# The u half of x times w_in as seven block products, with x kept whole in float32

## The chip, the cores and the metric

The kernel runs on one core of a Trainium2 chip. The metric is the device time of one execution in microseconds (us). The kernel before takes 490.66 us, the median of three runs from 490.58 to 491.45. The profile is one more execution, which took 491.71 us, of which the traced span is 489.9 us.

## The reference

An attention without a softmax over the products gives x, and a gated feed-forward block with a spatial gate takes x on. There are 8 batches (b), 576 positions, 8 heads of 64 channels (512 in all), and a hidden width of 1024, which splits into a u half and a v half of 512.

```
q = softmax(q, channels);  k = softmax(k, positions)
x[b] = q (k^T v)                         # [576, 512], heads side by side
h = gelu_tanh(x @ w_in)                  # w_in [512, 1024]
u, v = h[:, :512], h[:, 512:]
v_n = (v - mean(v)) / sqrt(var(v) + 1e-6) * g_ln
v_s = w_sg @ v_n + b_sg                  # over positions, w_sg [576, 576]
out = x + (u * v_s) @ w_out              # w_out [512, 512]
```

## The kernel before, in words

Every large product runs in TensorE's fp32r type and keeps float32's precision by splitting each operand into a high part (rounded to fp32r) and a low part (the rest): high x high, low x high and high x low are summed in PSUM. A product thus costs three passes.

All of x, u and the output lie transposed, channels on partitions, positions along the free axis. Per batch, the steps are:

- `x_kv b` (L685): x of batch b from its q and k^T v, into three PSUM tiles, and then k^T v of batch b+1 (`kv_all`). ACT's `x_high` casts x from PSUM to its high part, DVE's `x_low` subtracts that from PSUM and leaves the low part. `x_h` and `x_l` have two buffers each, so that two batches may be in flight.
- `hv_mm b i` (L747): one 128-row tile of the v half, 12 matmuls of 512 columns. There are nine of these for each pair of batches: the last 64 rows of two batches share the fifth tile of the even one. Then `hv_gelu`, `hv_sq`, `hv_stat`, `hv_pow`, `hv_norm` and the split `hv_high`, `hv_low`.
- `hu_mm b f` (L813), four of them: a 128-row tile of the u half, 4 blocks of 128 input channels x 3 passes x 2 halves of 288 positions = 24 matmuls of 128x288. `hu_gelu` follows on ACT.
- `sg_mm b d` (L821), four of them, 28 matmuls of 128x288; `gate` (DVE) multiplies with u, `gate_high` (ACT) and `gate_low` (DVE or POOL) split the result.
- `out_mm b e` (L850), four of them, 24 matmuls of 128x288. `out_add` (DVE, L856) adds the high part of x from the PSUM result into a tile `o`, `out_rest` (DVE or POOL, L862) adds the low part, `out_store` sends it off.

Beside this run the softmaxes of q and k of later batches (`q_max` to `q_turn`, `k_sub`, `k_exp`, `kt_max`) on DVE, ACT and POOL, and, in batch 0 and 1 only, a finer start-up form of the same steps and the splitting of the weights (`wi_*`, `ws_*`, `wo_*`).

What sets the order is a text, `PLAN` (L34 to L131): steps are issued one by one in its order, and each engine keeps the order in which it was given its instructions. An engine that waits for one instruction therefore holds back all that is behind it. Two-bank PSUM tiles (`ps2`, three of them) go round among x, u, sg and out results, one-bank tiles (`ps1`, two) among v tiles and k^T v. All matmuls are issued by one helper (L238), all other instructions by another (L151), so rows are told apart by tile names.

Of the kernel before, what the change touches and what calls it, by code (L numbers as in the profile page):

```python
# [957 lines left out]
```

## Time and profile before

| what | value |
|---|---|
| median of 3 runs | 490.66 us (490.58 to 491.45) |
| the profiled execution | 491.71 us, traced span 489.9 us |
| PE busy | 483.5 us, 99% of the span |
| DVE, ACT, POOL busy | 334.8 us (68%), 240.3 us (49%), 162.2 us (33%) |
| granted TensorE clock | 0.999 of full speed, mean |

The page names the busy time of each engine, then the span in 40 slices, the chain that ended last and the costliest groups. PE is busy in all but the first and the last slice. What an instruction of a group takes is its mean; its record can overlap with that of the instruction behind it, so the spacing of starts is less than the mean.

### The profile page before, as it was taken

How to read it: one execution, taken by the hardware profiler on the slowest of the kernel's cores; microseconds unless marked ns; L12 is line 12 of the kernel's file. 1: busy time of each engine (PE TensorE's matmuls, PEld its weight loads, DVE VectorE, ACT ScalarE, POOL GpSimd, SP SyncE). 2: the span in 40 equal slices, each digit the busy share in tenths (PEclk: the TensorE clock that was granted, in tenths of full speed). 3: DMA queues.
4: the chain of work that ended last, by engine and by line, in shares of the span. 5: the costliest groups of instructions: out<-in, count | busy, mean ns of one | idle time of the engine just before them, and what ended most of it. 6: DMA issues, size and time to landing. Idle time of an engine off the chain costs nothing.

```text
span 489.9 us, 9391 instructions
## 1 busy us (share of the span) xinstructions
PE 483.5 (99%) x3885; PEld 446.9 (91%) x3885; DVE 334.8 (68%) x530; ACT 240.3 (49%) x398; POOL 162.2 (33%) x173
## 2 busy tenths in 40 slices
PE   8999999999999999999999999999999999999997
PEld 6698789999899889998899989999899979999997
DVE  8999898788578875896666687586156663426162
ACT  4899777732645657354625583356415154221220
POOL 4214423662425242751442701333023320114030
PEclk9999999999999999999999999999999999999999
DMA  8995741454147231544802243114000010000102
GB/s 301 359 403 217 277 118 65 143 199 105 63 141 286 80 131 47 160 136 161 251 27 98 98 135 118 30 74 128 0 27 0 25 74 0 1 2 24 50 25 97
DMA packets 20637, 57.28 MB, mean 117 GB/s; under 512 B 3057, under 2 KB 3569, under 8 KB 20594
## 3 DMA queue, kind: packets, MB, share of 16 engines
q1 hardware_dynamic: 20594, 56.68, 33.9%
q8 instruction: 30, 0.49, 0.4%
q14 instruction: 13, 0.11, 0.1%
HBM read 47.22 MB, written 9.45 MB: 116 GB/s over the span
## 4 chain that ended last, share of the span: by engine, by line
PE 92%; DVE 4%; ACT 2%; issue 1%; DMA 1%; POOL 0%; ACTq 0%
PE ps L238 92%; DVE o L151 1%; DVE vnl L151 1%; DMA qq<-q 1%; ACT qq L151 1%; DVE wi_l L151 0%; ACT qs L151 0%; DVE qm L151 0%; ACT x_l L151 0%; DVE qq L151 0%; POOL qq L151 0%; ACT o L151 0%; DVE wi_h L151 0%; DVE qd L151 0%; DVE qt L151 0%
## 5 line engine op out<-in xcount | busy, mean ns | idle before, releaser
L151 DVE TENSOR_TENSOR u<-ps,u 128x576 f32<-128x576 f32 x32 | 24.1, 754 | 57.3 <-PE ps L238 48.6
L151 ACT CAST gh<-u 128x576 fp32r<-128x576 f32 x32 | 21.1, 675 | 78.1 <-DVE u L151 78.0
L238 PE MATMUL ps<-ulow,wo_h 128*128 128x288 f32 (+1 forms) x260 | 56.5, 295 | 0.0
L238 PE MATMUL ps<-gh,wo_l 128*128 128x288 f32 (+1 forms) x260 | 56.4, 294 | 0.0
L238 PE MATMUL ps<-gh,wo_h 128*128 128x288 f32 (+1 forms) x260 | 56.3, 294 | 0.0
L238 PE MATMUL ps<-ws_h,vnl 128*128 128x288 f32 x256 | 54.9, 296 | 0.7 <-DVE vnl L151 0.7
L238 PE MATMUL ps<-ws_h,vnh 128*128 128x288 f32 x256 | 55.0, 296 | 0.0
L238 PE MATMUL ps<-ws_l,vnh 128*128 128x288 f32 x256 | 54.9, 296 | 0.0
L151 ACT ACTIVATE u<-ps 128x576 f32<-128x576 f32 (+2 forms) x36 | 21.0, 599 | 63.9 <-PE ps L238 59.7
L151 POOL TENSOR_TENSOR ulow<-u,gh 128x576 fp32r<-128x576 f32 x16 | 24.2, 1516 | 72.6 <-DVE ulow L151 43.7
L151 POOL TENSOR_TENSOR rs<-ve,half 128x1 f32<-128x1 f32 x36 | 27.9, 780 | 50.6 <-DVE ve L151 50.2
L238 PEld LDWEIGHTS ps<-gh,wo_h 128*128 128x128 f32 x260 | 42.4, 188 | 0.7
L238 PE MATMUL ps<-x_h,wi_h 128*128 128x288 f32 (+2 forms) x256 | 41.9, 299 | 0.3 <-ACT x_l L151 0.3
L238 PEld LDWEIGHTS ps<-ws_h,vnl 128*128 128x128 f32 x256 | 41.3, 188 | 0.9 <-DVE vnl L151 0.9
L238 PEld LDWEIGHTS ps<-gh,wo_l 128*128 128x128 f32 x260 | 42.1, 188 | 0.0
L238 PEld LDWEIGHTS ps<-ws_h,vnh 128*128 128x128 f32 x256 | 41.6, 188 | 0.5
L238 PEld LDWEIGHTS ps<-ulow,wo_h 128*128 128x128 f32 x260 | 42.0, 189 | 0.0
L238 PEld LDWEIGHTS ps<-ws_l,vnh 128*128 128x128 f32 x256 | 41.3, 188 | 0.0
L238 PE MATMUL ps<-x_h,wi_l 128*128 128x288 f32 (+2 forms) x256 | 41.3, 296 | 0.0
L238 PE MATMUL ps<-x_l,wi_h 128*128 128x288 f32 (+2 forms) x256 | 41.2, 296 | 0.0
L151 ACT ACT_TABLE_LOAD x30 | 38.5, 1283 | 5.4 <-DMA qq<-q 3.9
L151 DVE SCALAR_TENSOR_TENSOR vnl<-v,rs,vnh 128x512 fp32r<-128x512 f32 x32 | 30.9, 972 | 14.9 <-ACT vnh L151 14.7
(119 smaller groups left out, 1038.0 us busy)
## 6 DMA issues: line engine op xcount, KB each, us to landing
vv<-v SPq DMA_DIRECT2D x16, 650.0 KB, 5.2
out<-o SPq DMA_DIRECT2D x31, 288.0 KB, 3.1
qq<-q SPq DMA_DIRECT2D x14, 576.0 KB, 4.2
kk<-k SPq DMA_DIRECT2D x12, 640.0 KB, 5.7
kmt<-kt SPq DMA_DIRECT2D x24, 288.0 KB, 3.9
ghws<-w_sg SPq DMA_DIRECT2D x5, 320.0 KB, 8.4
kmt<-scr SPq DMA_DIRECT2D x6, 256.0 KB, 4.2
ukt<-kt SPq DMA_DIRECT2D x4, 288.0 KB, 6.5
```

The lines of the kernel that those rows point to most:

```text
L151: ins = op(*args, **kw)
L238: tc.keep_in_program_order(nc.tensor.matmul(*args, **kw))
```

## The change

It has four parts.

First, from batch 2 on the u half is no longer four `hu_mm` but seven block products in Winograd's form of Strassen's method. x (512 channels x 576 positions) and the u half of w_in (512 x 512) are cut in 2 x 2 blocks. Four sums of weight blocks are formed once, while batch 1 runs (`sw_get`, `sw_add`, `sw_high`, `sw_low`), and four sums of x blocks for each batch (`d_add` on DVE, `d_high` on ACT, `d_low` on DVE). `us_mm b n` (n = 1 to 7) is one product of 2 x 2 x 3 = 12 matmuls of 128x288, each with its own stationary operand. Products 1 and 2 add up in PSUM tile `ua`, 5 and 3 in `uc`, and 6, 7 and 4 in `ub`. DVE's `us_add` reads `ub` after product 6, after 7 and after 4, and `uc` after 5 and after 3, each time before the next product is added on top. `us_one` (ACT) copies product 1 before product 2 goes on top. Four `us_gelu` follow instead of four `hu_gelu`.

Second, x is copied from PSUM to a float32 tile `xf` (`x_get`, `x_tail`, ACT; two buffers, by the parity of the batch), and `x_high` and `x_low` work from that tile. `out_add` adds the output into `xf` in place, `out_rest` and `both` are gone, and the store reads `xf`. The high and low parts of x have one buffer each. For batch 0, `x_sum` forms `xf` from the two parts.

Third, the memory for this comes from other tiles: the x sums live in `u` (whole), in `gh`, `qq` and a new tile `sd` (parts); `sd` also holds the weight sums and half of what `gate_low` writes. Odd batches no longer have their last 64 positions in front.

Fourth, `PLAN` is new from its row 14 on.

```diff
-hv_pow 3 0, q_top 5 0, out_store 1 2, out_mm 2 2, load_kt 6 1, out_add 2 2, out_rest 2 2 V, load_kt 6 2, kt_max 6 1, load_kt 6 3, hu_mm 3 1
...
+d_low 3 1, x_get 4 1, us_mm 3 1, q_turn 5 0, us_mm 3 6, hv_stat 3 2 A, d_high 3 3, d_low 3 3, us_one 3, d_low 3 4, hv_pow 3 2, hv_high 3 2, us_mm 3 5
...
-    x_h, x_l = (slots(n, 2, [P, NP, S + TL], F32R) for n in ("x_h", "x_l"))
-    u_s = slots("u", 5, [P, S])
+    xx_h, xx_l = (sb(n, [P, NP, S + TL], F32R) for n in ("x_h", "x_l"))
+    xf_s = [sb(f"xf{i}", [P, NP, S]) for i in range(2)]
+    uu_s = slots("u", 2, [P, 2, S])
...
-    sq = sb("sq", [P, DV])
...
-    o_all = sb("o", [P, ST, S])
...
+    def xf(b):
+        return xf_s[b % 2]
+    def u_s(b, f, at=None):
+        return uu_s(b, f // 2, at=f // 2)[:, f % 2]
+    def sd_all():
+        return late("sd", [P, 12 * DH + 4 * HS])
...
+    def x_get(b, h, E=A):
+        copy(E, xf(b)[:, 2 * h:2 * h + 2, 0:ST * P], st[f"x{h}", b])
+    def x_tail(b, E=A):
         ps = st["xt", b][:, :, 0:2 * TL].rearrange("p z (h n) -> p z h n", h=2)
-        yield ps, x_tile(x, b)[:, :, where(b)[1]].rearrange("p (h z) n -> p z h n", z=2)
-        if b % 2:
-            yield ps, x(b - 1)[:, :, S:S + TL].rearrange("p (h z) n -> p z h n", z=2)
+        copy(E, xf(b)[:, :, ST * P:S].rearrange("p (h z) n -> p z h n", z=2), ps)
...
+    def x_sum(h, E=V):
+        hs = slice(2 * h, 2 * h + 2)
+        E.tensor_tensor(out=xf(0)[:, hs], in0=f32(xx_h[:, hs, 0:S]), in1=f32(xx_l[:, hs, 0:S]), op=ALU.add)
     def x_high(b, h):
-        ps, to = x_main(x_h, b, h)
-        A.copy(out=to, in_=ps)
-    def x_low(b, h):
-        (ps, to), (_, hi) = x_main(x_l, b, h), x_main(x_h, b, h)
-        V.tensor_tensor(out=to, in0=ps, in1=f32(hi), op=ALU.subtract)
+        hs, n = slice(2 * h, 2 * h + 2), S if b > 1 else ST * P
+        A.copy(out=xx_h[:, hs, 0:n], in_=xf(b)[:, hs, 0:n])
+    def x_low(b, h, E=V):
+        hs, n = slice(2 * h, 2 * h + 2), S if b > 1 else ST * P
+        E.tensor_tensor(out=xx_l[:, hs, 0:n], in0=xf(b)[:, hs, 0:n], in1=f32(xx_h[:, hs, 0:n]), op=ALU.subtract)
...
     def x_endh(b):
-        for ps, to in x_ends(x_h, b):
-            A.copy(out=to, in_=ps)
-    def x_endl(b):
-        for (ps, to), (_, hi) in zip(x_ends(x_l, b), x_ends(x_h, b)):
-            V.tensor_tensor(out=to, in0=ps, in1=f32(hi), op=ALU.subtract)
...
+    def w_parts(n):
+        if n == 3:
+            return w_block(1, 0)
+        z = sd_all()[:, 0:12 * DH].rearrange("p (k t c n) -> p k t c n", k=3, t=2, c=2)
+        return [z[:, {1: 0, 2: 1, 4: 2}[n], t] for t in range(2)]
...
+    def sw_add(n, E=V):
+        a, b, op = {
+            1: (w_whole(1, 0), w_whole(1, 1), ALU.add),
+            2: (w_sum(1), w_whole(0, 0), ALU.subtract),
+            3: (w_whole(0, 0), w_whole(1, 0), ALU.subtract),
+            4: (w_whole(0, 1), w_sum(2), ALU.subtract),
+        }[n]
+        E.tensor_tensor(out=w_sum(n), in0=a, in1=b, op=op)
...
+    def d_parts(b, n):
+        if n == 1:
+            z = sd_all()[:, 12 * DH:].rearrange("p (t c n) -> p t c n", t=2, c=2)
+        elif n == 3:
+            z = qq_s("d", b, n, at=1, shape=[P, 2, 2, HS], dt=F32R)
+        else:
+            z = gh_s("d", b, n, at=n // 2 - 1, shape=[P, 2, 2, HS])
+        return [z[:, t] for t in range(2)]
...
+    def d_sum(b, n):
+        return uu_s("d", b, n % 2, at=n % 2, shape=[P, 2, 2, HS])[:, (n - 1) // 2]
+    def d_add(b, n, E=V):
+        x, y = {
+            1: lambda: (x_block(b, 0, 1), x_block(b, 0, 0)),
+            2: lambda: (x_block(b, 1, 1), d_sum(b, 1)),
+            3: lambda: (x_block(b, 1, 1), x_block(b, 0, 1)),
+            4: lambda: (x_block(b, 1, 0), d_sum(b, 2)),
+        }[n]()
+        E.tensor_tensor(out=d_sum(b, n), in0=x, in1=y, op=ALU.subtract)
+    def d_high(b, n):
+        A.copy(out=d_parts(b, n)[0], in_=d_sum(b, n))
+    def d_low(b, n, E=V):
+        hi, lo = d_parts(b, n)
+        E.tensor_tensor(out=lo, in0=d_sum(b, n), in1=f32(hi), op=ALU.subtract)
...
+    def us_mm(b, n):
+        def xs(i, j):
+            return [block(z, j, i, HS) for z in (xx_h, xx_l)]
+        l, r, name, first = {
+            1: (w_block(0, 0), xs(0, 0), "ua", True),
+            2: (w_block(0, 1), xs(1, 0), "ua", False),
+            3: (w_parts(4), xs(1, 1), "uc", False),
+            4: (w_block(1, 1), d_parts(b, 4) if n == 4 else None, "ub", False),
+            5: (w_parts(1), d_parts(b, 1) if n == 5 else None, "uc", True),
+            6: (w_parts(2), d_parts(b, 2) if n == 6 else None, "ub", True),
+            7: (w_parts(3), d_parts(b, 3) if n == 7 else None, "ub", False),
+        }[n]
+        if first:
+            bank(ps2, name, b)
+        for s in range(2):
+            fs, m = slice(s * P, s * P + P), 0
+            for p, q in ((0, 0), (1, 0), (0, 1)):
+                for c in range(2):
+                    mm(st[name, b][:, s, 0:HS], l[p][:, c, fs], r[q][:, c], start=first and m == 0, stop=m == 5, skip_group_check=not first)
+                    m += 1
+    def u_block(b, i, j):
+        return uu_s(b, i, at=i)[:, :, j * HS:j * HS + HS]
...
+    def us_add(b, n, E=V):
+        of, one, to = {
+            6: ("ub", (1, 0), (0, 1)), 5: ("uc", (1, 0), (1, 1)), 7: ("ub", (1, 1), (1, 1)),
+            3: ("uc", (0, 1), (0, 1)), 4: ("ub", (1, 0), (1, 0)),
+        }[n]
+        E.tensor_tensor(out=u_block(b, *to), in0=us_sum(b, of), in1=u_block(b, *one), op=ALU.add)
+    def us_gelu(b, i, j):
+        z = u_block(b, i, j)
+        A.activation(z, z if i or j else us_sum(b, "ua"), AF.Gelu_apprx_tanh)
...
+    def gate_rest(b, d):
+        if d < 2:
+            return sd_all()[:, 12 * DH + d * S:12 * DH + d * S + S]
+        return uu_s("low", b, at=0, dt=F32R)[:, d - 2]
...
+        E.tensor_tensor(out=gate_rest(b, d), in0=u_s(b, d), in1=f32(gated(b, d)), op=ALU.subtract)
...
     def out_add(b, e):
-        if b == B - 1:
-            V.tensor_tensor(out=split(o_s(b, e)), in0=st["o", b, e][:, :, 0:HS], in1=split(o_s(b, e)), op=ALU.add)
-            return
-        V.tensor_tensor(out=split(o_s(b, e, at=4 * b + e)), in0=st["o", b, e][:, :, 0:HS], in1=f32(split(x_h(b)[:, e, 0:S])), op=ALU.add)
-    def out_rest(b, e, E=G):
-        o = o_s(b, e)
-        E.tensor_tensor(out=o, in0=o, in1=f32(x_l(b)[:, e, 0:S]), op=ALU.add)
+        o = split(xf(b)[:, e])
```

Three places in the order of the instructions. On PE, batch 3, where the u half is computed (`x_h`, `x_l` are the parts of x, `wi_h`, `wi_l` those of w_in, `ghd_3_2` and `qqd_3_3` the x sums 2 and 3, `sd` the weight sums and x sum 1); before:

```order
L238 MATMUL ps2_0_78<-ulow_2_3_2369,wo_h_853 128x288 x2
L238 MATMUL ps2_0_78<-gh2_1_2363,wo_l_854 128x288 x2
L238 MATMUL ps2_1_79<-x_h3_2010,wi_h_61 128x288 x8
L238 MATMUL ps2_1_79<-x_h3_2010,wi_l_62 128x288 x8
L238 MATMUL ps2_1_79<-x_l3_2027,wi_h_61 128x288 x8
L238 MATMUL ps2_2_80<-x_h3_2010,wi_h_61 128x288 x8
L238 MATMUL ps2_2_80<-x_h3_2010,wi_l_62 128x288 x8
L238 MATMUL ps2_2_80<-x_l3_2027,wi_h_61 128x288 x8
```

and now, products 1, 6, 5 and the start of 7:

```order
L246 MATMUL ps2_0_80<-x_h_74,wi_h_61 128x288 x2
L246 MATMUL ps2_0_80<-x_h_74,wi_l_62 128x288 x2
L246 MATMUL ps2_0_80<-x_l_75,wi_h_61 128x288 x2
L246 MATMUL ps2_0_80<-x_h_74,wi_h_61 128x288 x2
L246 MATMUL ps2_0_80<-x_h_74,wi_l_62 128x288 x2
L246 MATMUL ps2_0_80<-x_l_75,wi_h_61 128x288 x2
L246 MATMUL ps2_1_81<-ghd_3_2_2541,sd_1062 128x288 x12
L246 MATMUL ps2_2_82<-sd_1062 128x288 x12
L246 MATMUL ps2_1_81<-qqd_3_3_2660,wi_h_61 128x288 x2
L246 MATMUL ps2_1_81<-qqd_3_3_2660,wi_l_62 128x288 x2
L246 MATMUL ps2_1_81<-qqd_3_3_2660,wi_h_61 128x288 x4
L246 MATMUL ps2_1_81<-qqd_3_3_2660,wi_l_62 128x288 x2
```

The two groups of 24 matmuls that stood in two PSUM tiles became groups of 12, with a second product going on top of the first in `ps2_1_81`.

On DVE at the same place (`kmt` is the k of batch 6, `vnl` and `v3` belong to the v half, `o` is the output tile); before:

```order
L151 TENSOR_TENSOR o_77<-ps2_0_78,x_h2_1625 128x576
L151 TENSOR_TENSOR o_77<-o_77,x_l2_1630 128x576
L151 TENSOR_REDUCE ktall_6_2501<-kmt_6_1_2536 128x1
L151 BN_STATS s63_1_2662<-v3_1_2387 128x6
L151 BN_AGGR mv3_1_2663<-s63_1_2662 128x2
L151 TENSOR_SCALAR ve3_1_2666<-mv3_1_2663 128x1
L151 SCALAR_TENSOR_TENSOR v3_1_2387<-v3_1_2387,mv3_1_2663,g_bc_67 128x512
L151 TENSOR_TENSOR o_77<-o_77,x_l2_1630 128x576
L151 TENSOR_TENSOR x_l4_2673<-ps2_0_78,x_h4_2655 128x2x512
```

and now, from x sum 2's low part (`ghd_3_2`) to the first `us_add` (last row):

```order
L160 TENSOR_TENSOR ghd_3_2_2541<-ud_3_0_2535,ghd_3_2_2541 128x576
L160 TENSOR_TENSOR ud_3_0_2535<-xf1_77,ud_3_0_2535 128x576
L160 TENSOR_REDUCE ktall_6_2281<-kmt_6_1_2532 128x1
L160 STREAM_TRANSPOSE qt5_0_2622<-qq5_0_2279 128x576
L160 SCALAR_TENSOR_TENSOR v3_2_2556<-v3_2_2556,nm3_2_2559,g_bc_67 128x512
L160 TENSOR_TENSOR qq5_0_2279<-qq5_0_2279,qd5_0_2391 128x576
L160 TENSOR_TENSOR sd_1062<-ud_3_1_2401,sd_1062 128x576
L160 STREAM_TRANSPOSE qt5_0_2622<-qq5_0_2279 128x576
L160 TENSOR_SCALAR ve3_2_2658<-sv3_2_2561 128x1
L160 TENSOR_TENSOR qqd_3_3_2660<-ud_3_1_2401,qqd_3_3_2660 128x576
L160 TENSOR_TENSOR ghd_3_4_2625<-ud_3_0_2535,ghd_3_4_2625 128x576
L160 TENSOR_TENSOR u3_0_2681<-ps2_1_81,u3_1_2663 128x2x288
```

The `us_add` of product 6 now stands behind five of the d steps, two norm and q steps and three transposes, where the output's two additions and statistics stood.

On PE after k^T v of batch 2 (`vv2`, `kk2`); before, the first u tile of batch 1 follows:

```order
L238 MATMUL ps1_1_82<-vv2_1_697,kk2_1_813 64x65 x8
L238 MATMUL ps1_0_81<-vv2_1_697,kk2_1_813 64x65 x8
L238 MATMUL ps2_0_78<-x_h1_729,wi_h_61 128x288 x8
L238 MATMUL ps2_0_78<-x_h1_729,wi_l_62 128x288 x8
L238 MATMUL ps2_0_78<-x_l1_733,wi_h_61 128x288 x8
L238 MATMUL ps2_1_79<-gh0_0_981,wo_h_853 128x288 x2
L238 MATMUL ps2_1_79<-ulow_0_0_1057,wo_h_853 128x288 x2
```

and now the first output tile of batch 0 (`gh0`, and `sd`, which `gate_low` writes on DVE):

```order
L246 MATMUL ps1_1_84<-vv2_1_845,kk2_1_888 64x65 x8
L246 MATMUL ps1_0_83<-vv2_1_845,kk2_1_888 64x65 x8
L246 MATMUL ps2_0_80<-gh0_0_1060,wo_h_920 128x288 x2
L246 MATMUL ps2_0_80<-sd_1062,wo_h_920 128x288 x2
L246 MATMUL ps2_0_80<-gh0_0_1060,wo_l_921 128x288 x2
```

The four u tiles of batch 1 moved behind all of batch 0's output and x of batch 2.

## Rows read from the trace of the kernel before

**Rows 1.** The page: busy time, share of the span and instructions by engine

```profile
PE 483.5 (99%) x3885; PEld 446.9 (91%) x3885; DVE 334.8 (68%) x530; ACT 240.3 (49%) x398; POOL 162.2 (33%) x173
```

**Rows 2.** What PE waited for, whole span: total, times, longest, us

```profile
PE ps L238 <- POOL vn L151: 1.3, 1, 1.3
PE ps L238 <- DVE vnl L151: 0.7, 1, 0.7
```

**Rows 3.** PE in order of time, u half of batch 3: start, length, operation

```profile
219.63 1.23 PE L238 MATMUL ps<-x_l,wi_h 128*128 128x288 f32 x8
220.70 1.23 PE L238 MATMUL ps<-x_h,wi_h 128*128 128x288 f32 x8
```

**Rows 4.** PE in order of time, first columns of the last output tile

```profile
476.37 0.29 PE L238 MATMUL ps<-gh,wo_h 128*128 128x288 f32 x1
...
477.97 0.43 PE L238 MATMUL ps<-gh,wo_h 128*128 128x288 f32 x2
```

**Rows 5.** PE in order of time, attention of batch 4, then a v tile

```profile
223.99 2.18 PE L238 MATMUL ps<-qt,kvt 64*64 64x512 f32 x32
225.99 2.43 PE L238 MATMUL ps<-vv,kk 64*64 64x65 f32 x80
228.35 1.34 PE L238 MATMUL ps<-x_h,wi_h 128*128 128x288 f32 x8
...
235.84 1.10 PE L238 MATMUL ps<-wi_h,x_l 128*128 128x512 f32 x4
236.77 1.09 PE L238 MATMUL ps<-wi_l,x_h 128*128 128x512 f32 x4
```

**Rows 6.** DVE by line and shape: count, busy us, mean ns, idle before

```profile
L151 DVE SCALAR_TENSOR_TENSOR vnl<-v,rs,vnh 128x512 fp32r<-128x512 f32 x32 | 30.9, 972 | 14.9 <-ACT vnh L151 14.7
...
L151 DVE TENSOR_TENSOR u<-ps,u 128x576 f32<-128x576 f32 x32 | 24.1, 754 | 57.3 <-PE ps L238 48.6 <-ACT u L151 8.7
...
L151 DVE STREAM_TRANSPOSE qt<-qq 128x576 f32<-128x576 f32 x28 | 21.3, 764 | 1.9 <-POOL qq L151 1.7
...
L151 DVE TENSOR_REDUCE ktall<-kmt 128x1 f32<-128x576 f32 x24 | 17.6, 743 | 3.4 <-DMA kmt<-kt 3.4
...
L151 DVE SCALAR_TENSOR_TENSOR v<-v,nm,g_bc 128x512 f32<-128x512 f32 x18 | 15.7, 876 | 2.9 <-ACT sq L151 2.9
...
L151 DVE TENSOR_TENSOR qq<-qq,qd 128x576 f32<-128x576 f32 x14 | 15.4, 1098 | 0.2
...
L151 DVE TENSOR_TENSOR ulow<-u,gh 128x576 fp32r<-128x576 f32 x16 | 12.0, 752 | 4.9 <-ACT gh L151 2.4 <-POOL ulow L151 2.3
...
L151 DVE TENSOR_TENSOR o<-o,x_l 128x576 f32<-128x576 f32 x14 | 11.7, 839 | 0.1
...
L151 DVE TENSOR_TENSOR qq<-qq,qm 128x1152 f32<-128x1152 f32 x7 | 9.5, 1352 | 0.2
...
L151 DVE TENSOR_TENSOR wi_l<-o,wi_h 128x512 fp32r<-128x512 f32 x2 | 1.4, 688 | 0.0
```

**Rows 7.** ACT by line and shape, the cast of a gated tile

```profile
L151 ACT CAST gh<-u 128x576 fp32r<-128x576 f32 x32 | 21.1, 675 | 78.1 <-DVE u L151 78.0
```

**Rows 8.** DVE in order of time, two instructions back to back

```profile
42.39 0.76 DVE L151 TENSOR_TENSOR qq<-qq,qd 128x576 f32<-128x576 f32 x1
43.07 0.68 DVE L151 BATCH_NORM_STATS2 s<-v 128x6 f32<-128x512 f32 x1
```

**Rows 9.** Busy time by stretch: PE, PEld, DVE, ACT, POOL, PEclk, DMA, GB/s

```profile
37.40:86.20 48.80, 48.80 (x368) 42.31 (x368) 45.61 (x74) 38.52 (x72) 19.26 (x23) 1.00 0.47 164
165.00:224.00 59.00, 59.00 (x479) 54.88 (x478) 45.12 (x69) 31.83 (x50) 27.54 (x32) 1.00 0.38 117
```

**Rows 10.** DVE by tile: shortest, median, longest ns, first and last start us

```profile
L151 DVE SCALAR_TENSOR_TENSOR vnl<-v,rs,vnh x32: 654/747/3550, 59.8 to 459.8; 128x512 fp32r<-128x512 f32 x32
...
L151 DVE TENSOR_TENSOR u<-ps,u x32: 720/758/759, 76.2 to 473.4; 128x576 f32<-128x576 f32 x32
...
L151 DVE TENSOR_TENSOR qq<-qq,qd x14: 742/758/1962, 42.4 to 385.2; 128x576 f32<-128x576 f32 x14
```

More of the change, by code (lines that the diff above doesn't have):

```diff
@@ new lines @@
+hv_stat 4 1 A, out_mm 3 2, out_add 3 2, q_mul 5 1 1, q_turn 5 3, k_exp 6 0, d_add 4 2, d_add 4 4, load_kt 7 2, hv_low 4 2, hv_pow 4 0, d_high 4 1
+load_kt 7 1, hv_mm 4 3, hv_gelu 4 3, hv_stat 4 3, hv_norm 4 3, kt_max 7 1, x_kv 5, x_get 5 0, out_store 3 2, x_tail 5, kv_inv 6 0, kv_scale 6 0
+x_endh 5, d_high 4 2, hv_high 4 0, hv_low 4 0, kt_max 7 2, us_mm 4 1, x_endl 5, hv_mm 4 4, d_high 4 3, x_get 5 1, d_low 4 1, hv_pow 4 3, d_high 4 4
+d_low 4 4, d_low 4 2, d_low 4 3, us_mm 4 6, us_mm 4 5, hv_gelu 4 4, us_one 4, load_kt 7 3, kt_max 7 3, us_add 4 6, us_mm 4 7, hv_stat 4 4, us_add 4 5
@@ new lines @@
+tail_low 5, hv_mm 5 2, hv_gelu 5 2, d_add 5 2, out_add 4 2, hv_low 5 0, q_turn 6 3, d_add 5 4, hv_stat 5 2, hv_norm 5 2, d_high 5 3, d_low 5 1
+hv_mm 5 1, hv_pow 5 2, hv_gelu 5 1, out_store 4 3, hv_stat 5 1, hv_pow 5 1, x_kv 6, hv_stat 5 3, hv_pow 5 3, hv_high 5 2, hv_low 5 2, kv_inv 7 1
+x_get 6 0, out_store 4 2, us_mm 5 1, hv_norm 5 1, d_high 5 2, x_get 6 1, us_mm 5 5, x_tail 6, d_low 5 3, hv_high 5 1, d_low 5 2, us_mm 5 6, q_top 7 0
+q_sub 7 0 V, d_high 5 4, d_low 5 4, us_one 5, us_add 5 5, us_add 5 6, us_mm 5 2, us_mm 5 7, us_gelu 5 0 0, hv_norm 5 3, us_add 5 7, us_mm 5 3
@@ new lines @@
+d_add 7 4, d_low 7 3, tail_low 7, d_low 7 2, d_high 7 4, out_add 6 1, hv_pow 7 0, hv_high 7 0, d_high 7 1, hv_mm 7 1, hv_gelu 7 1, d_low 7 1
+hv_stat 7 1, us_mm 7 1, us_one 7, d_low 7 4, us_mm 7 6, hv_low 7 0, us_mm 7 5, tail_again 7, hv_pow 7 3, hv_high 7 3, us_add 7 6, hv_pow 7 1
+us_mm 7 2, us_gelu 7 0 0, hv_norm 7 1, hv_high 7 1, us_mm 7 7, us_add 7 5, out_store 6 1, us_add 7 7, us_mm 7 3, us_add 7 3, us_gelu 7 1 1
+us_gelu 7 0 1, hv_low 7 1, us_mm 7 4, us_add 7 4, us_gelu 7 1 0, hv_low 7 3, sg_mm 7 0, gate 7 0, gate_high 7 0, sg_mm 7 1, gate 7 1, sg_mm 7 2
@@ L250, in gmlp_kernel @@
     raw = {}
-    for n in ("vnh", "vnl", "wo_h", "wo_l", "x_h", "x_l"):
-        two = pool.tile([P, 2, 4, P, 2], U32, name=f"raw_{n}", tag=f"{n}1" if n[0] == "x" else n)
-        kind = "o" if n[0] == "x" else "i"
-        raw[kind, sum(z[0] == kind for z in raw)] = two
+    for i, n in enumerate(("vnh", "vnl", "wo_h", "wo_l")):
+        raw["i", i] = pool.tile([P, 2, 4, P, 2], U32, name=f"raw_{n}", tag=n)
+    four = pool.tile([P, 4, 4, P, 2], U32, name="raw_o", tag="sd")
+    for i in range(2):
+        raw["o", i] = four[:, 2 * i:2 * i + 2]
     wide = {}
@@ L688, in x_kv, with halves @@
             kv_all(b + 1)
-    def halves(z, o=0):
-        return [z[..., o:o + HS], z[..., o + HS:o + S]]
-    def where(b):
-        o = b % 2 * TL
-        return slice(o, o + ST * P), slice(ST * P, S) if not o else slice(0, TL)
+    def halves(z):
+        return [z[..., 0:HS], z[..., HS:S]]
     def x_mm(b):
@@ L701, in x_mm @@
             bank(ps2, n, b)
-        main, last = where(b)
+        main, last = slice(0, ST * P), slice(ST * P, S)
         for h in range(2):
```

259 lines of the change are left out of this document (139 added, 120 removed).

## The prediction

> **What bounds the kernel now.** I read the busy shares first, then what TensorE (PE) waits for, then PE in order of time, and last VectorE (DVE), by tile and by stretch. The reader is to see in the shares [rows 1] that PE is busy for 483.5 us of a span of 489.9 and DVE for 334.8. The waits [rows 2] show the two that stand on another engine, 1.3 and 0.7 us: nothing that PE needs comes late. The granted clock is 0.999. So the span is the number of matmuls times their pace, and a matmul less is time less as long as its successors' operands are ready.
>
> The pace: eight matmuls of 128x288 take 220.70 − 219.63 = 1.07 us [rows 3], 0.133 us each. There two neighbours share a stationary operand. In the first columns of the last output tile twelve matmuls, each with its own stationary operand, start over 477.97 − 476.37 = 1.60 us [rows 4], also 0.133 each. The new products load a weight block for each matmul, as the second case does; PEld is below PE even in the sum (446.9 against 483.5, same count [rows 1]). I take 0.133 for both.
>
> **The matmuls.** Per batch from 2 on, four u tiles of 24 matmuls become seven products of 12: 96 to 84. Over six batches 72 matmuls are gone: 72 x 0.1333 = **−9.60 us**. All of these lie on PE's path. Nothing else on PE changes in number.
>
> **What DVE gets.** Per batch four d_add, four d_low and five us_add; once twelve steps on the weight sums and two x_sum. There is no row for them, so the nearest ones price them [rows 6]. The d_low are a subtraction of a high part from SBUF as `ulow` is, 0.752 us; I take that for d_add, too, 48 x 0.752 = 36.1 us. us_add reads PSUM and SBUF as `u<-ps,u` does, 0.754: 30 x 0.754 = 22.6. Weight sums as `wi_l`, 0.688: 8.3. x_sum as the widest, 1.352: 2.7. Off come 14 second output additions of 0.839, 11.7. The sum is +58 us: 334.8 becomes some 393, 81% of a span near 483. ACT gains some 40 us (24 d_high at 0.675 [rows 7] are 16 of it; the rest are x copies from PSUM and us_one, priced alike) and reaches 280, 58%. Neither is a bound as a share. But PE has no slack, so what counts is each place where PE needs a DVE result that stands far back in DVE's order. Two such places come out of the order.
>
> **Place one: the first output of batch 0.** Before, u tiles of batch 1 stood on PE between k^T v of batch 2 and the first output matmul; now that matmul follows at once, and needs the low part that `gate_low` of tile 0 writes on DVE. From DVE's first step on k^T v of batch 1 to that gate_low, 59 instructions stand in DVE's order. Their lengths, each by its group in [rows 6], add to 44.2 us. Back to back a start follows the last one sooner than its length: 42.39 to 43.07 is 0.68 for a length of 0.76 [rows 8], 0.08 less. Some 40 of the 59 follow without waiting, 40 x 0.08 = 3.2: 41.0. PE beside it has 18 u matmuls (18 x 0.133 = 2.4), one x (225.99 − 223.99 = 2.0), six v tiles (each 3 x 0.93 = 2.80 [rows 5], together 16.8), four sg tiles of 28 matmuls (112 x 0.133 = 14.9), one k^T v (228.35 − 225.99 = 2.36 [rows 5]): 38.5, and I add 0.5 for starts and ends: 39.0. PE waits **+2.0 us** here. Bounds: if all 59 are spaced by 0.08 less, 39.5 − 39.0 = 0.5; if none, 5.2. That DVE is tight in this stretch is seen without counting: between 37.40 and 86.20 it is busy for 45.61 of 48.80 us already [rows 9], and the weight sums and x_sum come on top. Most of the time in which u of batch 1 used to cover it is kept, since those matmuls only move behind; it is the cover that goes, not work.
>
> **Place two: each product block.** After batch b−1's last output PE has a v tile (2.80), an x (2.00), k^T v (2.36), then products 1, 6, 5 and 7 of 12 x 0.133 = 1.60 each. Product 7 goes on top of 6 in the same PSUM tile, so it can only start when us_add of product 6 has read that: at 2.80 + 2.00 + 2.36 + 3 x 1.60 = 11.96 us. Behind the last output addition DVE has 15 instructions in batch 3 before that us_add: seven like those above (7 x 0.752 = 5.26), three transposes (3 x 0.764 = 2.29), a maximum (0.743), a norm (0.876), a q product (1.098), a 64-row low part (taken at 0.972, as `vnl`), all by [rows 6]: 11.24. A 128x1 step I leave out. With 0.08 off each it is 10.1. us_add itself takes 0.75, so it ends between 10.9 and 12.0 against 11.96: just in time or some 0.1 late. Later us_add (7, 5, 3, 4) have one or two short steps ahead of them for products of 1.60. Batch 2 and 7, walked in the same way, keep 0.3 to 1 us. I take 0.2 a block, **+1.2 us** for six. Below it is 0; above it is 1.5 a block, 9, if DVE is held up as told next.
>
> What speaks against the price of the d steps is another row. Among DVE's instructions with both inputs from SBUF, `vnl` has a median of 747 ns, a mean of 972 and a longest of 3550, and the q product a median of 758 and a longest of 1962, while `u<-ps,u`, with one input from PSUM, never takes over 759 in 32 [rows 10]. `ulow`, with two from SBUF, has a mean of 752 over 16 [rows 6], so this is not so everywhere. The excess of `vnl` is 972 − 747 = 225 ns on average. All d steps and the low part of x (which now reads SBUF, not PSUM) are of the exposed kind; the us_add are not. By the mean excess each block would have 7 x 0.225 = 1.6 us more ahead of its us_add. I stay at 0.752, since the row that matches in operation and shape has it.
>
> The Trainium skill has a rule for this, "SBUF — State Buffer", in "Who interferes with whom": a VectorE instruction with two SBUF inputs contends with a GpSimd instruction that reads SBUF, and whoever starts first has the shared interface for its whole length. The long tails in [rows 10], and their absence where one input is from PSUM, agree with it; by it the sum would come out by the rival "DVE held up" below.
>
> **What hides the rest.** The copies of x to float32 and d_high are on ACT, at 58%. x_h and x_l now have one buffer: the copy for batch b+1 must wait for the last product of batch b that reads x; between it and the next use of x stand four sg, four output tiles on PE (28 x 0.133 x 4 + 24 x 0.133 x 4 = 27.7 us), which hides two casts and two subtractions (below 5 us). The output is added into xf, so the store holds xf for a batch; with two of them that is a batch of PE's time. POOL loses its 14 second additions and becomes freer. The last output tile, its addition and store are as before. I cost these at nothing; if a cover fails, it is 1 to 2 us a batch.
>
> **The sum** on the profiled execution: 491.71 − 9.60 + 2.0 + 1.2 = 485.3. That execution is 491.71 − 490.66 = 1.05 above the median, so I forecast **484.3 us**, −1.3%.
>
> **Rivals.** *DVE late more often* (still faster): place one costs its upper bound, 5.2, and each block 0.5, 3.0 in all: 490.66 − 9.60 + 8.2 = 489.3. For it: 11.24 and 44.2 at full lengths, which leave no slack. Against it: DVE is at 45.12 of 59.00 us in a later stretch [rows 9], so what it is late by is made up before the next block.
>
> *The gain is eaten*: waits of 8.6 to 10.6 us, 489.7 to 491.6.
>
> *DVE held up* (slower): the steps with two SBUF inputs are stretched as `vnl` is. Place: the us_add of product 6 in every block. Price: 7 x 0.225 = 1.6, of which 1.5 reaches PE, six times, 9.0, and 5.2 at place one: −9.60 + 14.2 = +4.6, 495.3. It decides once PE's new waits exceed 9.6 us in all, 1.6 a block or 0.7 with place one at its bound. For it: the tails in [rows 10]; against it: `ulow`'s 0.752, and POOL works less than before.
>
> *The change does not do what it says*: matmuls with own stationary operands at a slower pace. At 0.15 us instead of 0.133 the 504 product matmuls would take 8.4 us more and eat the gain; [rows 4] speak against it directly. It is in the chance of the gain being eaten.
>
> **How the numbers follow.** The forecast has 0.66, DVE late more often 0.15, the gain eaten 0.06, DVE held up 0.13. The forecast's own range: with no new wait 490.66 − 9.60 = 481.1, and half of the 0.7 us wait on `vnl` [rows 2] gone, 480.7; with place one at 5.2 and the blocks at 0.2 in all, 486.5. The time is in 480.7 to 489.7 in some 8 of 10, the upper end where the second rival ends and the third begins. A measurement of this kernel can tell some 0.2%, 0.98 us: faster 0.66 + 0.15 = 0.81, the same 0.06, slower 0.13.
>
> **What would show it.** Right: PE's matmul count down by 72, products spaced by 1.60 us, PE busy near 474, a wait of PE for a DVE low part at about 90 us of 0.5 to 5, and waits on us_add below half a microsecond a block. DVE at some 390 us. Wrong: d_add or d_low with a mean of 0.9 or more, and PE waiting more than a microsecond for us_add in each block; or a wait for x's high or low part, which I cost at nothing; or products at a slower pace than 1.60.

## The result and the profile after

The changed kernel takes 485.03 us, the median of four runs from 483.99 to 487.01, against 491.06 for the kernel before on the same chips: a ratio of 0.9882 with an interval of 0.9846 to 0.9919. It is faster, by 6.0 us, and 0.7 above the forecast. A second set, beside the experiments, gave 485.30 against 490.77, 0.9894 (0.9878 to 0.9911).

One thing is needed to read these numbers. Of the eight executions in the two sets four have a mean granted clock of 1.000 and lie at 483.99 to 484.88 us, and four have 0.996 and lie at 485.71 to 487.01. The profiled execution is the slowest of the latter: 487.01 us, span 485.1.

The busy shares of the page, which answer to [rows 1]:

```profile
PE 477.0 (98%) x3813; PEld 438.4 (90%) x3813; DVE 376.1 (78%) x604; ACT 275.8 (57%) x441; POOL 140.6 (29%) x157
```

PE has 3813 matmuls, 72 less, as worked out, and is busy for 477.0 us, where I had put some 474. VectorE has 376.1 us, not 393. What PE waited for, over the whole span (us in total, times, longest), answers to [rows 2]:

```profile
PE ps L246 <- DVE qt L160: 1.5, 1, 1.5
PE ps L246 <- POOL vn L160: 1.3, 1, 1.3
PE ps L246 <- DVE xf L160: 0.7, 1, 0.7
```

No row names `u`, `ghd`, `qqd` or the weight sums: PE waits for no product's operand and for no us_add. The wait on `vnl` is gone. Two waits are new, on a transpose of q and on an output addition, and neither is in the prediction.

PE in order of time in batch 3, products 6, 5 and the start of 7 (start, length, operation); it answers to [rows 3]:

```profile
226.90 1.75 PE L246 MATMUL ps<-ghd,sd 128*128 128x288 f32 x12
228.48 1.76 PE L246 MATMUL ps<-sd 128*128 128x288 f32 x12
230.09 0.43 PE L246 MATMUL ps<-qqd,wi_h 128*128 128x288 f32 x2
```

Twelve matmuls start over 1.58 and 1.61 us: the forecast pace of 0.133 holds with a stationary operand each. VectorE by line and shape (count, busy us, mean ns, idle before), which answers to [rows 6]:

```profile
L160 DVE TENSOR_TENSOR u<-ps,u 128x576 f32<-128x576 f32 x62 | 46.2, 752 | 35.8 <-PE ps L246 33.1 <-ACT u L160 2.2
L160 DVE SCALAR_TENSOR_TENSOR vnl<-v,rs,vnh 128x512 fp32r<-128x512 f32 x32 | 23.6, 745 | 6.9 <-ACT vnh L160 6.8
L160 DVE TENSOR_TENSOR qq<-qq,qd 128x576 f32<-128x576 f32 x14 | 10.5, 752 | 0.2
L160 DVE TENSOR_TENSOR ud<-xf,ud 128x576 f32<-128x576 f32 x12 | 9.0, 749 | 1.9 <-PE ps L246 1.7
L160 DVE TENSOR_TENSOR ghd<-ud,ghd 128x576 fp32r<-128x576 f32 x12 | 8.9, 749 | 0.0
L160 DVE TENSOR_TENSOR xf<-x_h,x_l 128x1152 f32<-128x1152 f32 x2 | 5.1, 2558 | 0.0
```

The d steps take 0.749 us, as priced. `vnl` fell from 972 to 745 and the q product from 1098 to 752, though the change does not touch them: 7.3 and 4.9 us of the 17 by which the forecast of VectorE's sum was too high. And one kind is far too long: x_sum, forecast at 1352 ns, has a mean of 2558. Its place in VectorE's order of time:

```profile
46.65 1.38 DVE L160 STREAM_TRANSPOSE qt<-qq 128x576 f32<-128x576 f32 x2
...
50.40 3.76 DVE L160 TENSOR_TENSOR xf<-x_h,x_l 128x1152 f32<-128x1152 f32 x1
54.09 1.42 DVE L160 STREAM_TRANSPOSE qt<-qq 128x576 f32<-128x576 f32 x2
```

POOL at that time:

```profile
50.27 2.68 POOL L160 TENSOR_TENSOR ws_l<-ghws,ws_h 128x1152 fp32r<-128x1152 f32 x1
```

and PE, which needs those transposes for the attention of batch 1:

```profile
52.27 1.09 PE L246 MATMUL ps<-qt,kvt 64*64 64x512 f32 x8
54.91 2.99 PE L246 MATMUL ps<-qt,kvt 64*64 64x512 f32 x24 [1.54 <-DVE qt L160]
57.82 1.77 PE L246 MATMUL ps<-wi_h,x_h 128*128 128x512 f32 x4
59.44 1.09 PE L246 MATMUL ps<-wi_h,x_l 128*128 128x512 f32 x4
```

The second x_sum starts at 50.40, just after POOL's ws_l, and ends at 54.16, 1.21 us after ws_l's end at 52.95. I call it held: as if it had to wait for POOL's instruction before doing its own work. PE stands still for 1.54 us, and the attention takes 57.82 − 52.27 = 5.55 us. The granted clock then falls, by stretch (PE, PEld, DVE, ACT, POOL busy, PEclk, DMA share, GB/s):

```profile
55.00:57.00 2.00, 2.00 (x12) 1.00 (x15) 2.00 (x3) 0.00 (x0) 0.00 (x0) 0.67 0.96 370
57.00:59.00 2.00, 2.00 (x18) 1.45 (x13) 2.00 (x4) 1.03 (x3) 0.00 (x0) 0.50 0.09 38
```

0.50 is the lower of the two levels, 1.2 GHz. This wait and this clock are what experiments e0 to e3 take apart; e5 to e7, e9 and e11 ask what the products are worth and how near VectorE is to their edge.

### The profile page after: what moved, and what is told of

It reads as the page before. It is cut to its first block, busy times and chain, and to the rows that moved or that the text cites. A ratio compares the mean times of both kernels' runs of the same rounds, so it can differ in the third digit from the quotient of the medians.

```text
span 485.1 us, 9360 instructions
## 1 busy us (share of the span) xinstructions
PE 477.0 (98%) x3813; PEld 438.4 (90%) x3813; DVE 376.1 (78%) x604; ACT 275.8 (57%) x441; POOL 140.6 (29%) x157
## 4 chain that ended last, share of the span: by engine, by line
PE 88%; DVE 6%; DMA 3%; ACT 2%; issue 1%; POOL 0%; SPq 0%; DVEq 0%; ACTq 0%
PE ps L246 88%; DVE xf L160 1%; DMA kk<-k 1%; DMA scr<-ktall 1%; DMA qq<-q 1%; DVE qd L160 1%; DVE kk L160 1%; DVE ktall L160 1%; ACT qq L160 1%; DVE wi_l L160 0%; DVE wo_l L160 0%; ACT kk L160 0%; DVE qm L160 0%; ACT qs L160 0%; DVE u L160 0%
## 5 line engine op out<-in xcount | busy, mean ns | idle before, releaser
L160 DVE TENSOR_TENSOR u<-ps,u 128x576 f32<-128x576 f32 x62 | 46.2, 752 | 35.8 <-PE ps L246 33.1
L160 DVE TENSOR_TENSOR xf<-ps,xf 128x576 f32<-128x576 f32 (+2 forms) x34 | 24.2, 716 | 26.8 <-PE ps L246 26.8
L246 PE MATMUL ps<-wi_h,x_h 128*128 128x512 f32 x144 | 40.3, 402 | 0.1
L246 PE MATMUL ps<-wi_l,x_h 128*128 128x512 f32 x144 | 39.6, 396 | 0.2 <-DVE wi_l L160 0.2
L246 PE MATMUL ps<-wi_h,x_l 128*128 128x512 f32 x144 | 39.4, 396 | 0.0
L160 ACT ACTIVATE v<-ps 128x512 f32<-128x512 f32 x36 | 21.4, 598 | 29.3 <-PE ps L246 28.2
L246 PEld LDWEIGHTS ps<-wi_l,x_h 128*128 128x128 f32 x144 | 27.0, 188 | 7.1 <-DVE wi_l L160 0.6
L246 PEld LDWEIGHTS ps<-wi_h,x_l 128*128 128x128 f32 x144 | 27.0, 188 | 6.5
L160 POOL COPY qe<-qd 32x36 f32<-32x36 f32 x44 | 14.4, 328 | 61.4 <-DVE qd L160 59.7
```

What stands on the lines that cost most here:

```text
L160: ins = op(*args, **kw)
L246: tc.keep_in_program_order(nc.tensor.matmul(*args, **kw))
```

## The experiments

All are timed beside the kernel before; e0 to e3, e4 to e7, and e9 to e11 each on one chip, e8 on a fourth. The kernel before takes 490.72 to 490.77 us on these four, so times of different chips are compared below.

**e0, the changed kernel again.**

> The changed kernel once more, beside the others. In its first profile VectorE's second x_sum lasts 3.76 us for some 1.35, PE waits 1.54 us for a transpose behind it and then runs for 3.4 us at half clock. If both come and go from run to run, executions split into some near 484 (clock 1.000) and some near 487 (clock 0.996); if not, all lie at one of the two.

Measured: 484.17, 485.71, 486.17 and 484.88 us, clocks 1.000, 0.996, 0.996 and 1.000. The profiled execution (484.17) has the wait and not the half clock. PE:

```profile
52.22 1.09 PE L246 MATMUL ps<-qt,kvt 64*64 64x512 f32 x8
54.85 1.97 PE L246 MATMUL ps<-qt,kvt 64*64 64x512 f32 x24 [1.54 <-DVE qt L160]
56.75 1.20 PE L246 MATMUL ps<-wi_h,x_h 128*128 128x512 f32 x4
57.79 1.09 PE L246 MATMUL ps<-wi_h,x_l 128*128 128x512 f32 x4
```

From the first attention matmul to the second third of the v tile it is 5.57 us here and 59.44 − 52.27 = 7.17 with the half clock: the clock costs 1.6 us. The wait is in both profiled executions, the half clock in one. They are 2.84 us apart: 1.6 is the clock, 0.7 the wait for an output addition, which e0's does not have. That the clock splits the other six in the same way is told by their mean clocks alone.

**e1, the second x_sum behind the transposes.**

```diff
-kv_scale 1 1, x_sum 1, q_turn 1 2, q_turn 1 3, q_max 2 0
+kv_scale 1 1, q_turn 1 2, q_turn 1 3, x_sum 1, q_max 2 0
```

> The second x_sum moved behind the two transposes that PE waits for. Hold theory (an instruction of VectorE with two SBUF inputs waits for POOL's instruction that is under way): x_sum starts near 51.8 us, is held to 52.95 by POOL's ws_l, ends near 54.2 as now. PE's wait of 1.54 and the half clock go (3.2 us), but VectorE's later work comes no earlier than now less its 1.8 us of idle time, so the first output tile's low part is ready near 90.8 while PE wants it near 89.9: a new wait of about 0.9. Some 484.7 against 487.0 for a disturbed run of the changed kernel. Rival (x_sum is long by itself, for its two inputs or for the transfers running then): 3.76 us from 51.8 on, low part near 92.2, a wait of 2.3, some 486.1.

Measured: 482.88 us (482.52 to 484.15), 0.9844 (0.9829 to 0.9859), clock 1.000 in all. VectorE and, below, POOL:

```profile
50.45 1.43 DVE L160 STREAM_TRANSPOSE qt<-qq 128x576 f32<-128x576 f32 x2
51.80 2.41 DVE L160 TENSOR_TENSOR xf<-x_h,x_l 128x1152 f32<-128x1152 f32 x1
```

```profile
50.32 2.67 POOL L160 TENSOR_TENSOR ws_l<-ghws,ws_h 128x1152 fp32r<-128x1152 f32 x1
```

x_sum began 1.4 us later and ended at the same time, 54.21, 1.22 after ws_l: its length is set by POOL's end, not by itself. No wait came up at the first output tile; I had not counted that the transposes ran in time that was lost before. It is 1.8 us faster than I expected. PE now waits 0.73 us for a low part of x (`x_l`) at 59.17, which VectorE writes further on in the same order; in e2 that wait is 0.91, in e3 0.24.

**e2, POOL's ws_l on VectorE, x_sum where it was.**

```diff
-wo_a 2, wo_b 2, ws_l 0
+wo_a 2, wo_b 2
-q_turn 1 3, q_max 2 0
+q_turn 1 3, ws_l 0 V, q_max 2 0
```

> x_sum stays where it is; POOL's ws_l, which runs beside it, goes to VectorE behind the transposes (1.34 us more there). Hold theory: x_sum lasts 1.35 us, no wait for the transpose, no half clock, low part of the first output tile near 89.7 when PE wants it at 89.9; 483.8. Rival (long by itself): x_sum stays near 3.7, the wait of 1.5 and the half clock stay, and VectorE is 1.34 later at the first output tile; 487 or more.

Measured: 483.02 us (482.90 to 483.13), 0.9842 (0.9827 to 0.9857). VectorE:

```profile
50.17 1.35 DVE L160 TENSOR_TENSOR xf<-x_h,x_l 128x1152 f32<-128x1152 f32 x1
51.44 1.43 DVE L160 STREAM_TRANSPOSE qt<-qq 128x576 f32<-128x576 f32 x2
```

The same instruction, at the same place, with the same inputs takes 1.35 us once POOL's is away. That shows the hold. The time is 0.8 us below the 483.8 expected.

**e3 and e11, the second x_sum on POOL.**

```diff
-kv_scale 1 1, x_sum 1, q_turn 1 2
+kv_scale 1 1, x_sum 1 G, q_turn 1 2
```

> The second x_sum on POOL, behind ws_l there, some 3 us; VectorE has 3.76 us less. Both theories: no wait for the transpose, clock 1.000, low part of the first output tile ready 1 us or more before PE wants it; 483.8, and every run near it. Slower than that only if VectorE's next instructions with two SBUF inputs (a norm near 55 us) are held by POOL's x_sum instead.

> e3 again, as the base of the two beside it: 482.0 to 482.9, clock 1.000 in all executions.

Measured: 482.16 (482.02 to 482.92), 0.9828 (0.9813 to 0.9842), and again 481.98 (481.86 to 482.44), 0.9823 (0.9810 to 0.9837); clock 0.999 to 1.000. This beats both kernels: some 3.1 us under the changed one, 8.6 and 8.75 under the one before. It is 1.6 us below the 483.8 expected, though the low part of the first output tile is ready only 0.6 us before PE starts on it, not 1 us. What PE waits for (e11, all rows):

```profile
PE ps L246 <- POOL vn L160: 1.3, 1, 1.3
PE ps L246 <- ACT x_l L160: 0.3, 1, 0.3
PE ps L246 <- ACT kk L160: 0.2, 1, 0.2
PE ps L246 <- DVE wi_l L160: 0.2, 1, 0.2
```

All of these lie in the first 40 us, and 490.73 − 9.60 = 481.13 is 0.85 us below 481.98: of the products' gain all but that is there, and no run takes the rest apart.

**e9, product 1 issued twice, on e3** (its sums start from zero again): `for s in range(4 if n == 1 else 2)`, then `s %= 2`.

> e3 with product 1 of each batch issued twice on PE, the second time from zero again (same result): 72 matmuls of 128x288 more, as many as the four u tiles had, and nothing else changed. If PE is the bound through every product block: + 72 x 0.1333 = 9.6 us over e3 (482.16), 491.8. If some of a block's time is a wait for VectorE that the 1.6 us more would cover: less, by up to 0.5 a block, 488.8 to 491.8.

Measured: 491.38 us (491.18 to 491.95) against 481.98 for e11: +9.40 for 72 matmuls, 0.131 us each. The price of the main term is shown on the chip, for matmuls that are added to the new order: no part of a product block is time in which PE waits for VectorE.

**e4, e8 and e10, four u tiles instead of the products, on e3.** In each the d, us and weight-sum steps are left out and `hu_mm b f`, `hu_gelu b f` stand in their places. In e4 the fourth tile of batch 4 stands behind the cast of half of batch 5's x into the same buffer and reads that, so e4 does not compute the same output.

> The changed kernel with the second x_sum on POOL (e3, 482.16 us), but with u from batch 2 on by the four u tiles of 24 matmuls again; all d, us and weight-sum steps are left out, x whole in float32 and the new order stay. If the products are worth what their matmuls are and wait for nothing: + 72 x 0.1333 = 9.6 us, 491.8. If VectorE's added work (58 us of d, us and weight sums) costs PE anything in the products, the step is smaller by that: 9.6 less 1 to 4.

> As e4 (e3 with four u tiles of 24 matmuls per batch from 2 on, without the d, us and weight-sum steps), but the four u tiles stand at the places of the first four products, ahead of the casts of the next batch's x, which in e4 overwrote x under the last u tile and made PE wait. If the products are worth their matmuls: 482.16 + 72 x 0.1333 = 491.8, plus what PE waits for in this order, which the waits show (0 to 3 us). If VectorE's added work costs PE something in the products: the matmuls' part is the same, but PE has fewer waits than e3, below 491.8.

> As e8, but each tile's gelu stands two products' places later, behind the copies of x that it held up on ACT there (PE waited 1.6 us three times for them, and some 11 us for parts of the v half behind the gelus). Matmuls alone: 482.16 + 9.6 = 491.8; with waits left in this order 492 to 498. Below 491.8 only if the products' VectorE work cost PE something.

Measured: 501.92, 516.17 and 506.20 us. They do not price the products, since this order does not suit the tiles: in e10 PE waits 5.4 us for `vnl` and 3.2 for `vnh`, parts of the v half that come late on ACT and VectorE, and the clock is 0.990. What they show is that four tiles cannot be put back in this order without a new one. e9 was made for this reason.

**e5, POOL's work put back, on e3.** A `G.tensor_tensor(out=o, in0=o, in1=zero.broadcast_to([P, S]), op=ALU.add)` behind 14 output additions.

> e3 with 14 additions of a zero to an output tile on POOL, behind the same 14 output additions behind which POOL had the second addition before (some 1.2 to 1.4 us each, two SBUF inputs; the value stays the same). Hold theory: instructions of VectorE with two SBUF inputs that last over 150 ns longer than their kind go from 6 to some 10 to 16, each ending a fixed time after POOL's; vnl's mean goes from 745 towards 850 to 970 ns; PE waits 0 to 4 us more, 482 to 486. Rival (vnl and the q product were long before for another reason): their means stay at 745 to 760 and the time at 482.2.

Measured: 491.41 us (490.93 to 492.23), clock 0.992 to 0.997: +9.3, where I had expected 0 to 4. Long instructions with two SBUF inputs rose from 6 to 14, each of them beside one of POOL's. But `vnl` stayed at 744 ns, so that number of mine was wrong, too, and most of the time went another way. POOL near 268 us:

```profile
267.59 1.53 POOL L160 TENSOR_TENSOR xf<-xf,zero 128x576 f32<-128x576 f32 x1 [7.61 <-issue]
269.08 2.97 POOL L160 TENSOR_TENSOR kk<-kk,kmt 128x1280 f32<-128x1280 f32 x1
272.01 1.15 POOL L160 TENSOR_TENSOR xf<-xf,zero 128x576 f32<-128x576 f32 x1
273.12 0.55 POOL L160 TENSOR_TENSOR rs<-ve,half 128x1 f32<-128x1 f32 x1
273.63 1.15 POOL L160 TENSOR_TENSOR qq<-qq,qd 128x576 f32<-128x576 f32 x1
```

The q product comes 2.7 us later, behind two additions, PE waits for its transpose (1.2 us) and for a gelu (2.1), and the clock falls to 0.50 for 281 to 284 us. So in this order POOL's queue has no room for the additions that the change removes; I had cost their removal at nothing. What they would cost in the old order this does not show.

**e6, every d_low twice, on e3** (`for _ in range(2):` ahead of it).

> e3 with every d_low issued twice (same result): 24 x 0.68 = 16.3 us more on VectorE, 2.7 in each product block, nothing on PE. By the prediction's walk (us_add of product 6 just in time) PE would wait some 2.5 us in each of six blocks: + 15, 497. By the gaps seen ahead of that us_add after the change (0.6 to 2.2 us in most blocks) some 1 to 2 a block: + 6 to + 12, 488 to 494. If VectorE's margin is larger than the gaps show: + 0 to 2.

Measured: 491.85 us (491.39 to 492.96): +9.7, within the second case. PE in batch 3:

```profile
225.71 1.10 PE L246 MATMUL ps<-sd 128*128 128x288 f32 x7
228.53 0.53 PE L246 MATMUL ps<-qqd,wi_h 128*128 128x288 f32 x2 [1.72 <-DVE u L160]
```

The us_add of product 6 is the edge, as the prediction said, but VectorE had about 1 us of margin there: of 2.7 us added, 1.72 came out.

**e7, k_sub of batch 3 on VectorE, on e3** (`k_sub 3 1 G` to `k_sub 3 1 V`).

> e3 with k_sub of batch 3's second half on VectorE instead of POOL: the two k_sub no longer run beside each other. Hold theory: VectorE's k_sub lasts 1.48 instead of 2.48 us, ahead of an output addition for which PE waited 0.7 us in the first profile of the change and an exponential for which it waited 0.2: 0.2 to 0.7 us less, 481.5 to 482.0. Rival: VectorE has 1.48 us more to do at a place where PE waits for it, 482.2 to 483.

Measured: 482.70 us (482.54 to 483.00), 0.9835 (0.9822 to 0.9848): no gain over e3, and where the rival had put it. VectorE's k_sub is no longer held, but PE had not waited for it in e3 any more.

## Why the prediction held, and which of its steps did not

**The matmuls, −9.60:** right. The pace is 0.133 us in the trace, and e9 measured 9.40 for 72.

**Place one, +2.0 (0.5 to 5.2):** this step failed. PE did not wait at the first output tile. VectorE writes the low part, and PE starts on it, at

```profile
91.77 0.75 DVE L160 TENSOR_TENSOR sd<-u,gh 128x576 fp32r<-128x576 f32 x1
```

```profile
93.10 0.42 PE L246 MATMUL ps<-sd,wo_h 128*128 128x288 f32 x2
```

that is 93.10 − 92.52 = 0.58 us after it is there. VectorE's busy time between the two ends of the walk (DVE busy, PEclk, DMA share, GB/s) is

```profile
49.30:92.52 43.22, 41.03 (x61) 0.96 0.46 154
```

41.03 us, against 41.0 forecast; but 2.41 of them are the hold of x_sum (3.76 − 1.35), and PE had by then lost time of its own. My sum was right by accident: without the hold it is 38.6. About half of the 2.4 us too many are long ones inside the means of [rows 6]: the stretch has four `vnl` at 0.75, priced there at 0.972, and two norms at 0.74, priced at 0.876, 1.2 us. PE's side was too short: in e11, where PE waits for nothing in this stretch, it goes from 49.30 to 89.47, 40.2 us against 39.0. So 38.6 stand against 40.2, not 41.0 against 39.0, and VectorE is not late. In e0 to e3 and e11, with the hold or without, it is the same 0.59 us ahead. My walk also left out that one of its steps, the gate of a spatial tile, waits for PE:

```profile
82.97 0.76 DVE L160 TENSOR_TENSOR u<-ps,u 128x576 f32<-128x576 f32 x1 [0.70 <-PE ps L246]
```

The same step waits 0.16 us in e1, e2, e3 and e11. From there to the low part the lead is the same in all six traces, whatever came before.

**Place two, +1.2:** wrong in size, by a small amount: nothing. In batch 3 VectorE runs from the last output addition to the us_add of product 6 as

```profile
218.14 0.76 DVE L160 TENSOR_TENSOR xf<-ps,xf 128x576 f32<-128x576 f32 x1 [1.60 <-PE ps L246]
...
227.43 0.75 DVE L160 TENSOR_TENSOR ghd<-ud,ghd 128x576 fp32r<-128x576 f32 x1
228.74 0.76 DVE L160 TENSOR_TENSOR u<-ps,u 128x576 f32<-128x576 f32 x1 [0.55 <-PE ps L246]
```

228.18 − 218.90 = 9.28 us, 0.24 of it a wait for ACT: 9.0 where I had 10.1 to 11.2, and then it waits 0.55 for PE. Three lengths were means with long ones in them: the q product at 1.098, the low part at 0.972 and the norm at 0.876 came in at 0.75 each, 0.70 less in all. And of the seven steps that I priced at 0.752 there are six in the order (two `ud`, two `ghd`, `sd`, `qqd`), 0.75 less.

**What stood in their place:** 4.1 us over the clean sum of 490.77 − 9.60 = 481.17, where I had 3.2. The hold of x_sum makes the wait of 1.54 us. The same attention and the start of the v tile in e11 are

```profile
52.29 2.18 PE L246 MATMUL ps<-qt,kvt 64*64 64x512 f32 x32
54.40 1.20 PE L246 MATMUL ps<-wi_h,x_h 128*128 128x512 f32 x4
55.44 1.09 PE L246 MATMUL ps<-wi_h,x_l 128*128 128x512 f32 x4
```

From the first attention matmul to the second third of the v tile it is 55.44 − 52.29 = 3.15 us, against 7.17 in the first profile and 5.57 in that of e0: the hold costs 4.0 us with the half clock and 2.4 without, 3.2 on average; the medians gave 3.1 (485.30 − 482.16). Some 1 us of the 4.1 is left, which no run takes apart. The other new wait, 0.7 for an output addition, stands behind a k_sub of 2.69 us on VectorE that ended 1.35 after POOL's k_sub; that wait is in the first profile and, as 0.80, in that of e1, not in those of e0, e3 and e11. The total was close because two waits that I forecast did not come and one that I had not placed did: that is luck.

**The other rivals:** VectorE was not late more often, the gain was not eaten, and the products did not run at a slower pace (1.58 to 1.61 us).

**The rival "VectorE held up":** its mechanism is real, its place was wrong. It did not fall on the d steps (0.749 us) but on x_sum, the one instruction that I took from the row of the widest without asking what POOL does then. The rows of before had it: `vnl` at 3550 ns [rows 10] stands in VectorE's order of before as

```profile
111.77 4.29 DVE L151 SCALAR_TENSOR_TENSOR vnl<-v,rs,vnh 128x512 fp32r<-128x512 f32 x2
```

with POOL beside it:

```profile
112.54 2.96 POOL L151 TENSOR_TENSOR kk<-kk,kmt 128x1280 f32<-128x1280 f32 x1 [2.97 <-issue]
```

It ends 116.06 − 115.50 = 0.56 us after POOL's, and the 0.7 us for which PE waited for `vnl` in [rows 2] end there:

```profile
116.11 0.53 PE L238 MATMUL ps<-ws_h,vnl 128*128 128x288 f32 x2 [0.67 <-DVE vnl L151]
```

I went through every instruction of VectorE that lasts over 150 ns longer than its kind: 18 before, 16.9 us too long in all; 7 after, 8.1 us. Every one of the 25 overlaps one of POOL's with two inputs, and ends a time after it that depends on its own shape alone: 0.06 for 36 columns, 0.55 for 512, 0.61 for 576, 1.21 for an addition or subtraction of 1152, 1.35 for 1280. So the tail in [rows 10] was no property of `vnl`; it was what POOL had under way. It did not leave with POOL's 14 additions: only 7 of the 18 end behind an output step that the change removes, the other 11 behind work that POOL still does, and e5 put 14 additions back without a long `vnl`. It left with the new order. Six of the 7 are still there in e11, and PE waits for none of them.

The traces also show the other side. Where VectorE's instruction started first, it kept its length and POOL's was stretched; before, VectorE and below POOL:

```profile
82.19 1.48 DVE L151 TENSOR_TENSOR kk<-kk,kmt 128x1280 f32<-128x1280 f32 x1
```

```profile
82.35 3.32 POOL L151 TENSOR_TENSOR qq<-qq,qm 128x1152 f32<-128x1152 f32 x1 [4.45 <-DVE qm L151]
```

The same subtraction on POOL takes 2.13 us at 214.16. The long `vnl` above is the one case in which VectorE's record starts first, by 0.04 us, and VectorE was held.

The Trainium skill, "SBUF — State Buffer", "🔬 SBUF: two separate sides", says that the shared interface is held for an instruction's whole length and not split. The held x_sum agrees: in the profile of the changed kernel and in e1 it ends 1.21 and 1.22 us after POOL's instruction, near the 1.35 that it takes with nothing beside it in e2.

The rival's price was too high by VectorE's margin. I had 1.5 of 1.6 us in each block reach PE; with the margin of about 1 us that e6 shows in batch 3, some 0.6 would have. It took e6's 2.7 us in each block to cost 9.7 us and so reach the time of before; that is the 1.6 us of PE's time in each block that I had named as the point of decision.

**What I cost at nothing:** x in single buffers and the output in place cost PE nothing in the profile of the changed kernel, as forecast. The removal of POOL's additions was not worth nothing: by e5 the new order loses 9.3 us with them, as much as the products' matmuls are worth, so the gain needs both. In the old order PE waited for nothing behind them [rows 2].

## What to carry to other kernels

Where a kind of instruction has a mean far above its median, take the median for the sum and look up what another engine does during the long ones: the excess moves with that engine's order, not with the instruction. Before a two-input step is given a place on VectorE, look at what POOL has under way there, and put one of the two elsewhere if a transpose or cast that PE needs stands behind it. When matmuls are taken from a PE that is busy for 99%, their count times their pace is the gain as long as nothing that PE needs comes later, and an added load on VectorE can be tested for its margin by doubling a harmless step.

## What the runs showed of the hardware that I had not expected

A wait of PE can cost more than itself. The 1.54 us of idle time among attention matmuls on 64 partitions cost 2.4 us in e0, where the clock stayed up: the 8 matmuls ahead of it and the 24 behind it take 1.09 + 1.90 us, and all 32 take 2.11 in e11. In the profiled execution of the changed kernel the granted clock then fell to 0.50, at a cost of another 1.6 us; in e0 it did not. Four of eight executions have that mean of 0.996. In the profiled execution of e6, PE stood still for up to 1.72 us among full 128x288 matmuls, and the mean clock is 0.999 to 1.000 in all eight executions; in that of e5 it fell to 0.50 after waits of 1.18 and 2.13 us. What tells the two apart, beyond what PE did around the wait, I did not test.
